# A spectral layer beside a gated linear unit on one Trainium2 core: operand addresses at multiples of 128 bytes, a written order for three engines, one load of x, and another spacing of the spectral tiles

## The chip, the cores and the metric

The kernel runs on one core of a Trainium2 chip. The metric is device time in microseconds (us) for one execution. The engines that matter here are TensorE (PE, matrix products; PEld is its loading of the stationary operand), VectorE (DVE), ScalarE (ACT), GpSimd (POOL, nearly unused) and SyncE (SP), whose queue issues nearly all DMA transfers.

## The reference

From x (2048 rows of 576 floats), normalised by row, two branches are computed and added to x. Everything is float32.

```python
def _A_ref(x, w_r, w_i):
    X = jnp.fft.rfft2(x, axes=(-2, -1))
    X = X * (w_r + 1j * w_i)
    return jnp.fft.irfft2(X, s=(S, D), axes=(-2, -1))

def _B_ref(x, w_gate, w_up, w_down):          # 576 -> 4608 -> 576
    g = jnp.einsum("bsd,df->bsf", x, w_gate)
    u = jnp.einsum("bsd,df->bsf", x, w_up)
    return jnp.einsum("bsf,fd->bsd", _sigmoid(g) * u, w_down)

xn = _layernorm(x, axis=-1)
return x + _A_ref(xn, A_w_r, A_w_i) + _B_ref(xn, B_w_gate, B_w_up, B_w_down)
```

## The kernel before

**Precision.** Each matrix product is made of three: every factor is cut into a rounded high part and a remainder, and high x high, low x high and high x low are accumulated. The high part is a copy on ACT (`hi`, `cut_hi`, `high`), the low part a subtraction on DVE that needs it (`lo`, `cut_lo`, `low`).

**First half: gate and up projections.** The 4608 hidden columns are 36 blocks f of 128. The rows of x are two halves p, each as two chunks of 512. The first two blocks are computed plainly (`plain`); from block 2 on a *unit* (f, p) computes a 2 x 2 block product with seven products P1 to P7 instead of eight (`unit`; `FACTORS` names their factors). A product is seven matmuls with a moving operand of 512 columns (`prod`, L373). The moving operands are the tiles X0... and X1... (halves p = 0 and 1), the stationary ones the weight tiles w. Three PSUM tags take the sums: `bA` and `bE` with two buffers, `bB` with one. The order in a unit: P1 of this unit was made ahead, in the unit before it; ACT copies `bA` to `bB` (L412); P5 to `bE`; P6 onto `bB`, ACT copies it to `h[:,0]` (L416); P2 onto `bA`, ACT takes its sigmoid (L419); P7 onto `bB`, ACT copies it to `h[:,1]` (L422), and DVE adds `bE` to that (L423); P1 of the next unit (`ahead`); P4 onto `bB`, sigmoid (L429); P3 onto `bE`, DVE adds it to `h[:,0]` (L432) and multiplies by the gates (L433). Between the products `beside()` takes one step each of side work written as generators: the weight tiles of the next block (`make_w`; two steps at a time in the units at which f changes, and finished at the fourth call), the sums of h and their store to scratch (`export`, L442), and the factors of w_down and their store to scratch (`make_t`: ACT copy L476, DVE subtraction L478, store L479, through a tile `tP` of tag `tt` with two buffers).

**Second half: down projection and the spectral branch.** The loop over `seq` has 252 steps n = (j, p, k): seven products j of the down projection (`ORDER`), two halves p, 18 blocks k. A step loads one scratch tile `sf` (`fetch`, ten steps ahead), cuts it into `sp` (L617, L621), and makes twelve matmuls `m` of 288 columns (`down`, L1008): four row tiles m by three partial products, with the factor tile `tt` as moving and `sp` as stationary operand. At the last k of a product `evac` adds the four PSUM tiles into the output accumulators `acc` (L946), and `landed` stores finished parts by way of `put` (one half of the rows from SP's queue, the other from ACT's, L711). Beside it the spectral branch runs in three stages of sixteen tiles each, generators again, one step per n (`aside`): `phase1b` (load x, normalise, fold, transposes `pf`, products `pd` and `pa`, store to scratch `sc1`), `phase2` (load from `sc1` and the filter weights w_r and w_i, products `pb` and `pc`, store to `sc2`), `phase3` (load from `sc2`, products `py`, transposes `pz`, products `pe`, added to `acc`). A tile of a stage begins every 4.36 steps, the stages at steps 2, 83 and 166. A tile has 26 matmuls in the first and third stage (six of them transposes) and twelve in the second; those that aren't transposes have 290 columns. Their PSUM tiles come from one tag with two buffers (`pair`). x is loaded twice: into `xb` for the spectral branch, and into `acc`, to which everything is added.

**Addresses.** Pools lie on the left or the right side of the on-chip memory. At the top of the right side stands an unused tile `edge` of eight floats (L155), and below it first `brief` and the X0 tiles, later the ring with `tt`, `sf` and `sp`. X1 and the weight tiles lie on the left. Spectral tiles are two rows of NP = 304 floats, of which 290 are used, so that a second row starts 1216 bytes after the first, nine and a half times 128.

**Order.** Only the opening, before the first plain blocks, is in an order written by hand (`manual_schedule`, DVE and ACT, L518). For all else a planner with its own estimate of durations fixes each engine's order when the kernel is compiled; on the chip an engine then takes its instructions in that order, whatever becomes ready first.

Of the kernel before, what the change touches and what calls it, by code (L numbers as in the profile page):

```python
# [9 lines left out]
F32 = mybir.dt.float32  # L10
# [10 lines left out]
NP = 304  # L21
# [103 lines left out]
def spectral_glu_kernel(ctx: ExitStack, tc: tile.TileContext, x, w_r, w_i, w_gate, w_up, w_down, out):  # L125
# [29 lines left out]
    ctx.enter_context(tc.tile_pool(name="edge", bufs=1, side="right")).tile([P, 8], F32, name="edge")  # L155
# [248 lines left out]
    def unit(u, beside, after):  # L404
# [58 lines left out]
    def make_t(k):  # L463
# [10 lines left out]
        def put(what, src):  # L474
# [5 lines left out]
            yield  # L480

# [141 lines left out]
    def early():  # L623
        for k in range(NPR):
            fetch_t(0, k)
            if k % 2 == 0 and k // 2 < FS:
                fetch(k // 2)
            if k >= 12:
                if k - 12 <= CA:
                    cut_hi(k - 12)  # L630
                if 0 <= k - 13 < CA:
                    cut_lo(k - 13)
            yield
        for n in range(FS, FA):
            fetch(n)
# [3 lines left out]
    make = iter(())  # L639
    for i, u in enumerate(UNITS):  # L640
        f, p = u
# [13 lines left out]
        def beside():  # L655
# [57 lines left out]
    def landed(t):  # L713
# [4 lines left out]
        if pending[t] == 0:  # L718
            put(t, slice(HD, D) if first_rows else slice(0, D))
# [7 lines left out]
    def wide(name, t, bufs=1, dtype=F32):  # L727
        return R["pool"].tile([P, 2, NP], dtype, tag=name, name=f"{name}{t}", bufs=bufs)[:, :, :NQ]

    def left_over(name, t):  # L730
        r = R["pool"].tile([P, 2, 112], F32R, tag=name, name=f"{name}{t}")[:, :, :3 * FR]
        return r, r.rearrange("p e (a b) -> p e a b", a=3)

    def phase1b(t):
# [9 lines left out]
        norm(xb[:, :D], xb[:, :D], t)  # L744
        eo = wide("eo", t)
# [3 lines left out]
        rows_, rp = left_over("rp", t)  # L749
# [30 lines left out]
        ah, al = wide("ah", t, 1, F32R), wide("al", t, 1, F32R)  # L780
# [12 lines left out]
        x1 = wide("x1", t)  # L793
# [3 lines left out]
    def phase2(i):  # L797
        pool, bm = R["pool"], R["bm"]
        kl = 2 * i
        x2 = wide("x2", i, 2)  # L800
        ws = []
        for nm, src in (("wr", w_r), ("wi", w_i)):
            w = pool.tile([P, 592], F32, tag=nm, name=f"{nm}{i}", bufs=2)[:, :2 * KD]
# [10 lines left out]
        h, l = wide("x2h", i, 1, F32R), wide("x2l", i, 1, F32R)  # L814
# [9 lines left out]
        sw, z, t2 = wide("sw", i), wide("z", i, 2), wide("t2", i)  # L824
# [20 lines left out]
        u = wide("u", i, 2)  # L845
# [3 lines left out]
    def phase3(t):  # L849
        pool, di = R["pool"], R["di"]  # L850
        u = wide("u3", t, 2)
# [7 lines left out]
        uh, ul = wide("uh", t, 1, F32R), wide("ul", t, 1, F32R)  # L859
# [10 lines left out]
        rows_, rp = left_over("rp3", t)  # L870
# [44 lines left out]
    def stage1():  # L915
        pool = room("1")
        R["cf"] = cf = pool.tile([P, 2, 5, NP], F32R, name="cf")
        load_r(cf, con["cf"].rearrange("p (e k n) -> p e k n", e=2, k=5))
        yield
# [20 lines left out]
    def evac(what, p, m, b):  # L940
        v = b[:, :HD]
        r1, r2 = acc[tid(p, 0, m)], acc[tid(p, 1, m)]
        c11, c12, c21, c22 = r1[:, :HD], r1[:, HD:], r2[:, :HD], r2[:, HD:]
# [4 lines left out]
        if what == "P1":  # L948
            U[p, m] = u = accp.tile([P, HD], F32, name=f"u{p}{m}")
            nc.scalar.activation(u, v, AF.Copy)  # L950
            add(c11, v)
        elif what == "P2":
            add(c11, v)
        elif what == "P6":
            add(U[p, m], v)
            add(c12, U[p, m])
        elif what == "P7":
            add(U[p, m], v)
            add(c21, U[p, m])
            add(c22, U[p, m])  # L960
        elif what == "P4":
            add(c21, v)
        elif what == "P5":
            w = accp.tile([P, HD], F32, tag="v", name=f"v{p}{m}", bufs=4)
            nc.scalar.activation(w, v, AF.Copy)
            add(c22, w)
            add(c12, w)
            landed(tid(p, 1, m))
        else:
            add(c12, v)  # L970
            landed(tid(p, 0, m))
# [6 lines left out]
    RATE = 4.36  # L978
    B1, B2, B3 = 2, 83, 166
# [72 lines left out]
```

## Time and profile before

| | us |
|---|---|
| median of 3 runs | 1471.11 (1470.16 to 1473.72) |
| profiled execution | 1470.79 |
| its span, first to last instruction | 1469.0 |
| first half, to the first `m` | 887.2 |
| second half, first `m` to the end of the last | 578.0 |
| from there to the last instruction | 3.8 |

The profile is of one execution. A line of a view names line, engine, operation and tiles; `x` is a count. In the table of stretches each engine has its busy time and, in brackets, its instructions; then follow the TensorE clock that was granted (1.00 is full), the mean busy share of the 16 DMA engines, and GB/s. In the waits stand the total, the times and the longest, in us. A matmul's recorded duration overlaps that of the next one, so rates are taken from start to start. On the timeline a row merges neighbours of one kind; its first number is the start, the second the time to the end of the last.

### The profile page before, as it was taken

Reading aid. Unit: us, or ns where it says so; the run is one execution under the profiler, and the core shown is the slowest. Engines: PE = TensorE matmul, PEld = TensorE weight load, DVE = VectorE, ACT = ScalarE, POOL = GpSimd, SP = SyncE. Lnnn points to the kernel's source line nnn. Section 1 sums busy time; section 2 is a strip of 40 time slices with the busy share of each in tenths; the row PEclk is TensorE's granted clock in tenths of the full one; section 3 lists DMA queues with packets and bytes.
Section 4 is the critical chain, followed back from the end, with each engine's and each line's share of the span. In section 5 each row is a group of like instructions: output and inputs, shape, how many; then the busy total and the mean of one; then the engine's idle time right before and its main releaser. Section 6 shows DMA issues by size and latency. Waiting matters only on the chain.

```text
span 1469.0 us, 22700 instructions
## 1 busy us (share of the span) xinstructions
PE 1409.5 (96%) x7804; PEld 1225.3 (83%) x7804; DVE 963.7 (66%) x1808; ACT 707.7 (48%) x1430; POOL 9.5 (1%) x36
## 2 busy tenths in 40 slices
PE   6999999999999999999999998999999999999998
PEld 4888777778777777788888887999999888999998
DVE  6877676758675766656556454666656777566664
ACT  6664454544444454434344332555544555555552
POOL 1000000000000000000000000000000000000000
PEclk9999999999999999999999999999999999999999
DMA  7235556555655565532333259887889999988863
GB/s 191 91 103 194 195 203 217 204 197 192 217 199 201 191 219 209 193 108 92 131 136 115 79 199 323 249 274 234 274 287 306 292 296 297 303 308 277 268 179 91
DMA packets 213619, 306.07 MB, mean 208 GB/s; under 512 B 20480, under 2 KB 98432, under 8 KB 213248
## 3 DMA queue, kind: packets, MB, share of 16 engines
q1 hardware_dynamic: 211440, 302.20, 63.2%
q10 hardware_dynamic: 2064, 2.43, 0.5%
q8 instruction: 61, 1.00, 0.3%
q14 instruction: 54, 0.44, 0.1%
HBM read 187.11 MB, written 117.44 MB: 207 GB/s over the span
## 4 chain that ended last, share of the span: by engine, by line
PE 51%; DVE 15%; DMA 15%; ACT 5%; issue 4%; SPq 4%; DVEq 0%; ACTq 0%
PE m L1008 17%; PE pB L373 11%; PE pE L373 7%; DMA ts<-tP 7%; PE pA L373 7%; DMA sf<-ss 2%; PE pd L778 2%; PE pe L903 2%; DVE w L231 2%; DVE h L433 2%; DMA ss<-h 2%; DVE tP L478 1%; SPq L205 1%; ACT ah L722 1%; DVE w L233 1%
## 5 line engine op out<-in xcount | busy, mean ns | idle before, releaser
L1008 PE MATMUL m<-tt,sp 128*128 128x288 f32 x3024 | 435.5, 298 | 10.7 <-ACT sp L617 7.6
L1008 PEld LDWEIGHTS m<-tt,sp 128*128 128x128 f32 x3024 | 412.1, 189 | 17.2 <-ACT sp L617 11.2
L621 DVE TENSOR_TENSOR sp<-sf,sp 128x512 fp32r<-128x512 f32 x252 | 169.6, 687 | 73.4 <-ACT sp L617 70.3
L617 ACT ACTIVATE sp<-sf 128x512 fp32r<-128x512 f32 x252 | 153.5, 627 | 96.4 <-PE m L1008 48.0
L373 PE MATMUL pA<-X0A,w 128*128 128x512 f32 x518 | 137.1, 400 | 1.8 <-DVE w L211 1.1
L227 ACT ACTIVATE w<-raw 128x384 fp32r<-128x384 f32 x238 | 111.1, 516 | 49.4 <-DVE raw L243 33.5
L373 PE MATMUL pA<-X1A,w 128*128 128x512 f32 x518 | 130.0, 391 | 0.0
L373 PE MATMUL pE<-X0S,w 128*128 128x512 f32 x490 | 125.8, 395 | 0.0
L373 PE MATMUL pB<-X0S,w 128*128 128x512 f32 x476 | 123.0, 396 | 2.7 <-ACT h L416 2.1
L373 PE MATMUL pE<-X1S,w 128*128 128x512 f32 x490 | 123.2, 391 | 0.2 <-DVE h L423 0.2
L373 PEld LDWEIGHTS pA<-X0A,w 128*128 128x128 f32 x518 | 97.7, 190 | 25.8 <-DVE w L211 1.6
L373 PE MATMUL pB<-X1S,w 128*128 128x512 f32 x476 | 119.1, 389 | 0.0
L478 DVE TENSOR_TENSOR tP<-wd,tP 128x288 fp32r<-128x288 f32 x126 | 56.7, 455 | 89.9 <-ACT tP L476 88.8
L373 PEld LDWEIGHTS pA<-X1A,w 128*128 128x128 f32 x518 | 97.1, 188 | 21.3
L373 PEld LDWEIGHTS pB<-X0S,w 128*128 128x128 f32 x476 | 88.4, 187 | 27.4 <-ACT h L416 3.4
L373 PEld LDWEIGHTS pE<-X0S,w 128*128 128x128 f32 x490 | 91.6, 187 | 21.8
L373 PEld LDWEIGHTS pE<-X1S,w 128*128 128x128 f32 x490 | 91.6, 188 | 21.1 <-DVE h L423 1.1
L476 ACT ACTIVATE tP<-wd 128x288 fp32r<-128x288 f32 x126 | 55.2, 442 | 108.1 <-DMA ts<-tP 86.6
L373 PEld LDWEIGHTS pB<-X1S,w 128*128 128x128 f32 x476 | 89.3, 188 | 18.8
L416 ACT ACTIVATE h<-pB 128x512 f32<-128x512 f32 x68 | 40.4, 594 | 131.0 <-PE pB L373 123.3
L423 DVE TENSOR_TENSOR h<-h,pE 128x512 f32<-128x512 f32 x68 | 46.5, 684 | 73.4 <-ACT h L422 73.1
L432 DVE TENSOR_TENSOR h<-h,pE 128x512 f32<-128x512 f32 x68 | 46.4, 683 | 72.4 <-PE pE L373 72.4
(186 smaller groups left out, 1876.9 us busy)
## 6 DMA issues: line engine op xcount, KB each, us to landing
sf<-ss SPq DMA_DIRECT2D x252, 256.0 KB
ss<-h SPq DMA_DIRECT2D x180, 256.0 KB
ts<-tP SPq DMA_DIRECT2D x126, 288.0 KB
tt<-ts SPq DMA_DIRECT2D x126, 288.0 KB
ss<-s SPq DMA_DIRECT2D x72, 256.0 KB
wd<-in_B_w_down SPq DMA_DIRECT2D x36, 288.0 KB
raw<-in_B_w_gate SPq DMA_DIRECT2D x72, 128.0 KB
raw<-in_B_w_up SPq DMA_DIRECT2D x72, 128.0 KB
```

The lines of the kernel that those rows point to most:

```text
L227: nc.scalar.activation(o[:, i, :3, :], src[:, i], AF.Copy)
L231: nc.vector.tensor_tensor(o[:, :, 3:, :], src[:, :, :KT, :], f32(o[:, :, :KT, :]), op=OP.subtract)
L373: nc.tensor.matmul(b, w[:, sw, :], xx[:, sx, :], start=start and j == 0, stop=stop and j == len(STEPS) - 1, skip_group_check=skip)
L416: nc.scalar.activation(h[:, 0], bB, AF.Copy)
L423: nc.vector.tensor_tensor(h[:, 1], h[:, 1], bE, op=OP.add)
L432: nc.vector.tensor_tensor(h[:, 0], h[:, 0], bE, op=OP.add)
L433: nc.vector.tensor_tensor(h, h, g, op=OP.mult)
L476: nc.scalar.activation(t[:, 0], src, AF.Copy)
L478: nc.vector.tensor_tensor(t[:, 1], src, f32(t[:, 0]), op=OP.subtract)
L617: nc.scalar.activation(s[:, 0], SF[n], AF.Copy)
L621: nc.vector.tensor_tensor(SP_[n][:, 1], SF[n], f32(SP_[n][:, 0]), op=OP.subtract)
L1008: nc.tensor.matmul(o, s[:, a, m * P:(m + 1) * P], t[:, b, :], start=k == 0 and i == 0, stop=k == NPR - 1 and i == 2)
```

## The change

- `edge` becomes 24 floats, and NP becomes 320, so that the tiles on the right side and the second rows of the spectral tiles start at multiples of 128 bytes. The tiles `wr`, `wi` and `xb` grow to 608 floats.
- From the third unit to the end PE, DVE and ACT issue in the order in which the program is written. SP's queue stays with the planner.
- With that, places in the written order move: the add of `bE` to `h[:,1]` behind the next unit's P1; one more step of pause in `make_t` after P2, P5 and P6; fewer double steps of `make_w`; the early fetches of `sf` ahead of those of `tt`; in the twin steps of `down` (the first two and the last two k) the matmuls of m = 0, 1 in the first of the two and those of m = 2, 3 in the second; the additions of `evac` over two steps, at the head of the step; P1's addition to `acc` put off to P2.
- `phase1b` loads x into `acc` alone, and normalises from there into one `xb` tile that is cleared once.
- Output stores go to SP's queue alone, but for the last ones.
- The stages begin at steps 3, 72 and 179, with a tile every 3.7, 6.2 and 3.75 steps; in the first and third the order of the tiles changes (upper rows first, then lower rows first).

```diff
-NP = 304
+NP = 320
...
-    ctx.enter_context(tc.tile_pool(name="edge", bufs=1, side="right")).tile([P, 8], F32, name="edge")
+    ctx.enter_context(tc.tile_pool(name="edge", bufs=1, side="right")).tile([P, 24], F32, name="edge")
...
         nc.scalar.activation(h[:, 1], bB, AF.Copy)
-        nc.vector.tensor_tensor(h[:, 1], h[:, 1], bE, op=OP.add)
         beside()
         if after:
             ahead(after)
+        nc.vector.tensor_tensor(h[:, 1], h[:, 1], bE, op=OP.add)
         beside()
...
             nc.sync.dma_start(tsp[ORDER.index(what)][k], f32(t).rearrange("p a d -> p (a d)"))
             yield
+            if what in ("P2", "P5", "P6"):
+                yield
...
+    written = ExitStack()
     for i, u in enumerate(UNITS):
+        if i == 2:
+            written.enter_context(tc.manual_schedule(engines={nc.tensor.engine, nc.vector.engine, nc.scalar.engine}))
...
-            for _ in range(2 if turn else 1):
+            for _ in range(2 if turn and (last or count < 4) else 1):
                 next(make, None)
                 next(soon, None)
             tick()
-            if turn and count == (7 if last else 4):
+            if turn and count == 7:
                 finish(make)
...
-    def put(t, cols):
+    def put(t, cols, both=False):
         for i, r in enumerate(rows(out, t)):
-            (nc.sync, nc.scalar)[i].dma_start(r[:, cols], acc[t][i * N1:(i + 1) * N1, cols])
+            (nc.scalar if both and i else nc.sync).dma_start(r[:, cols], acc[t][i * N1:(i + 1) * N1, cols])
...
-        xb = pool.tile([P, 592], F32, tag="xb", name=f"xb{t}", bufs=2)[:, :D + 2]
-        load_x(xb[:, :D], t)
-        nc.gpsimd.memset(xb[:, D:], 0.0)
+        acc[t] = accp.tile([P, D], F32, name=f"acc{t}")
+        pending[t] = 2
+        load_x(acc[t], t)
+        xb = R["xb"]
...
-        norm(xb[:, :D], xb[:, :D], t)
-        eo = wide("eo", t)
+        norm(xb[:, :D], acc[t], t)
+        eo = wide(pool, "eo", t)
...
         if what == "P1":
             U[p, m] = u = accp.tile([P, HD], F32, name=f"u{p}{m}")
             nc.scalar.activation(u, v, AF.Copy)
-            add(c11, v)
         elif what == "P2":
-            add(c11, v)
+            add(part(0), v)
+            yield
+            add(part(0), U[p, m])
...
-    RATE = 4.36
-    B1, B2, B3 = 2, 83, 166
...
-    for base, phase, n in ((B1, phase1b, HALVES * TPH), (B2, phase2, N2 // 2), (B3, phase3, HALVES * TPH)):
-        for t in range(n):
-            at(base + int(t * RATE), lambda t=t, phase=phase: phase(t))
...
+    UPPER = [tid(p, 0, m) for p in range(HALVES) for m in range(TPC)]
+    LOWER = [tid(p, 1, m) for p in range(HALVES) for m in range(TPC)]
+    for base, rate, stage, phase, ts in ((3, 3.7, stage1, phase1b, UPPER + LOWER), (72, 6.2, stage2, phase2, range(N2 // 2)),
+                                         (179, 3.75, stage3, phase3, LOWER + UPPER)):
+        at(base - 2, stage)
+        for i, t in enumerate(ts):
+            at(base + int(i * rate), lambda t=t, phase=phase: phase(t))
...
-    for i, n in enumerate((0, 3, 6, 9, 13, 17, 21, 25, 32, 40, 48, 56, 64, 72, 80, 88)):
-        t = tid(i // TPC % 2, i // TPH, i % TPC)
-        acc[t] = accp.tile([P, D], F32, name=f"acc{t}")
-        pending[t] = 2
-        loads.setdefault(n, []).append(lambda t=t: load_x(acc[t], t))
...
-            evac(ORDER[j], p, m, M[m])
+            done.append(evac(ORDER[j], p, m, M[m], n == len(seq) - 1))
+
+    done, out_of = [], []
+
+    def emptied():
+        out_of[:] = [g for g in out_of if next(g, out_of) is not out_of]
+        out_of.extend(g for g in done if next(g, done) is not done)
+        done.clear()
...
-        twin = k in (0, NPR - 2)
-        for m in range(TPC):
-            if k not in (1, NPR - 1):
+        emptied()
+        if k in (0, NPR - 2):
+            for m in range(2):
                 down(n, m)
-            if twin:
                 down(n + 1, m)
+        elif k in (1, NPR - 1):
+            for m in range(2, TPC):
+                down(n - 1, m)
+                down(n, m)
+        else:
+            for m in range(TPC):
+                down(n, m)
         active.extend(b() for b in begin.pop(n, []))
         aside()
```

More of the change, by code (lines that the diff above doesn't have):

```diff
@@ L623, in early @@
     def early():
[L624 to L632, printed above, removed]
+        for n in range(20):
+            if n < 2:
+                for i in range(3):
+                    fetch(3 * n + i)
+            else:
+                fetch_t(0, n - 2)
+            if 12 <= n <= 12 + CA:
+                cut_hi(n - 12)
+            if 13 <= n < 13 + CA:
+                cut_lo(n - 13)
             yield
@@ L718, in landed @@
         if pending[t] == 0:
-            put(t, slice(HD, D) if first_rows else slice(0, D))
+            put(t, slice(HD, D) if first_rows else slice(0, D), both)
     def hi(o, src):
@@ L725, in lo, with wide, left_over @@
         nc.vector.tensor_tensor(o, src, f32(h), op=OP.subtract)
[L727 to L731, printed above, removed]
+    def wide(pool, name, t, bufs=1, dtype=F32):
+        return pool.tile([P, 2, NP], dtype, tag=name, name=f"{name}{t}", bufs=bufs)[:, :, :NQ]
+    def left_over(pool, name, t):
+        r = pool.tile([P, 2, 112], F32R, tag=name, name=f"{name}{t}")[:, :, :3 * FR]
         return r, r.rearrange("p e (a b) -> p e a b", a=3)
@@ L792, in phase1b @@
         yield
-        x1 = wide("x1", t)
+        x1 = wide(pool, "x1", t)
         hi(x1, pa[:, :, :NQ])
@@ L799, in phase2 @@
         kl = 2 * i
-        x2 = wide("x2", i, 2)
+        x2 = wide(pool, "x2", i, 2)
         ws = []
         for nm, src in (("wr", w_r), ("wi", w_i)):
-            w = pool.tile([P, 592], F32, tag=nm, name=f"{nm}{i}", bufs=2)[:, :2 * KD]
+            w = pool.tile([P, 608], F32, tag=nm, name=f"{nm}{i}", bufs=2)[:, :2 * KD]
             v = src.rearrange("(k kl) n -> k (kl n)", kl=N2)[:, kl * KD:(kl + 2) * KD]
@@ L918, in stage1 @@
         load_r(cf, con["cf"].rearrange("p (e k n) -> p e k n", e=2, k=5))
+        R["xb"] = xb = pool.tile([P, 608], F32, name="xb")[:, :D + 2]
+        nc.gpsimd.memset(xb[:, D:], 0.0)
         yield
@@ L938, in spectral_glu_kernel, with evac, part @@
     U = {}
-    def evac(what, p, m, b):
+    def evac(what, p, m, b, both):
         v = b[:, :HD]
-        r1, r2 = acc[tid(p, 0, m)], acc[tid(p, 1, m)]
-        c11, c12, c21, c22 = r1[:, :HD], r1[:, HD:], r2[:, :HD], r2[:, HD:]
+        t1, t2 = tid(p, 0, m), tid(p, 1, m)
+        def part(q):
+            return acc[(t1, t2)[q // 2]][:, q % 2 * HD:(q % 2 + 1) * HD]
         def add(o, a):
@@ L950, in evac @@
             nc.scalar.activation(u, v, AF.Copy)
-            add(c11, v)
         elif what == "P2":
-            add(c11, v)
+            add(part(0), v)
+            yield
+            add(part(0), U[p, m])
         elif what == "P6":
             add(U[p, m], v)
-            add(c12, U[p, m])
+            yield
+            add(part(1), U[p, m])
         elif what == "P7":
             add(U[p, m], v)
-            add(c21, U[p, m])
-            add(c22, U[p, m])
+            yield
+            add(part(2), U[p, m])
+            add(part(3), U[p, m])
         elif what == "P4":
-            add(c21, v)
+            add(part(2), v)
         elif what == "P5":
@@ L965, in evac @@
             nc.scalar.activation(w, v, AF.Copy)
-            add(c22, w)
-            add(c12, w)
-            landed(tid(p, 1, m))
-        else:
-            add(c12, v)
-            landed(tid(p, 0, m))
+            yield
+            add(part(3), w)
+            landed(t2)
+            add(part(1), w)
+        else:
+            add(part(1), v)
+            landed(t1, both)
+        yield
     active = []
```

25 lines of the change are left out of this document (13 added, 12 removed).

## The prediction

> **What bounds the kernel now.** I read the page from the top, then the table of stretches, the waits, and the timeline where they fall.
>
> ```profile
> span 1469.0 us, 22700 instructions
> PE 1409.5 (96%) x7804; PEld 1225.3 (83%) x7804; DVE 963.7 (66%) x1808; ACT 707.7 (48%) x1430; POOL 9.5 (1%) x36
> ```
>
> TensorE (PE) is busy 96% of the span, DVE 66%, ACT 48%. So the end moves by two things alone: how far apart matmuls start when nothing is missing, and PE's waits. The profiled execution took 1470.79 us, 1.79 us more than its span; the median of three runs is 1471.11, so the sum below, made against 1470.79, stands 0.3 us under the median.
>
> ```profile
> core 0: us, PE busy (x) PEld busy (x) DVE busy (x) ACT busy (x) POOL busy (x), PEclk, DMA share, GB/s
> 110.00:886.00 776.00, 757.74 (x3253) 606.96 (x3252) 507.12 (x822) 341.71 (x688) 0.10 (x1) 1.00 0.51 177
> 650.00:850.00 200.00, 200.00 (x869) 162.48 (x868) 117.95 (x169) 79.24 (x151) 0.00 (x0) 1.00 0.34 118
> 886.00:920.00 34.00, 28.69 (x198) 27.87 (x198) 14.48 (x25) 9.16 (x18) 0.20 (x2) 0.90 0.99 309
> 920.00:1000.00 80.00, 76.64 (x562) 73.74 (x561) 50.54 (x102) 44.31 (x105) 0.69 (x7) 1.00 0.84 259
> 1000.00:1080.00 80.00, 76.07 (x557) 73.03 (x555) 53.46 (x109) 44.24 (x100) 0.60 (x6) 1.00 0.84 261
> ...
> 1115.00:1150.00 35.00, 31.78 (x228) 30.43 (x227) 24.07 (x52) 18.84 (x32) 0.00 (x0) 1.00 1.03 309
> 1150.00:1200.00 50.00, 45.93 (x318) 43.59 (x317) 36.05 (x78) 26.67 (x45) 0.00 (x0) 0.97 0.99 294
> 1200.00:1270.00 70.00, 65.24 (x462) 61.96 (x462) 52.09 (x112) 40.05 (x70) 0.00 (x0) 1.00 0.96 289
> 1270.00:1330.00 60.00, 60.00 (x453) 59.51 (x452) 35.61 (x66) 30.97 (x64) 0.00 (x0) 1.00 0.92 322
> 1330.00:1400.00 70.00, 70.00 (x536) 70.00 (x535) 47.30 (x93) 39.68 (x87) 0.00 (x0) 1.00 0.80 261
> ```
>
> Four stages show. The units (to 886) leave PE idle 776.00 - 757.74 = 18.3 us, none of it from 650 to 850. Stage 1 of the second half (to about 1110) takes 160 us for 562 + 557 = 1119 matmuls, 143 ns each; stage 2 (1115 to 1270) 155 us for 1008, 154 ns each, with the DMA engines full (0.96 to 1.03); stage 3 needs 70.00 / 536 = 130.6 ns and waits for nothing.
>
> ```profile
> PE pB L373 <- ACT h L422: 15.6, 18, 1.7
> PE pf L759 <- DVE eo L747: 11.2, 12, 5.3
> PE m L1008 <- ACT sp L617: 7.6, 13, 1.4
> ...
> PE pB L373 <- ACT h L416: 2.1, 3, 1.1
> PE m L1008 <- DVE u L946: 1.8, 2, 1.4
> ```
>
> Those are PE's own waits that matter (total, times, longest). The first, on the timeline:
>
> ```profile
> 611.92 0.44 ACT L476 ACTIVATE tP<-wd 128x288 fp32r<-128x288 f32 x1 [4.24 <-DMA ts<-tP]
> 612.27 0.58 ACT L419 ACTIVATE g<-pA 128x512 f32<-128x512 f32 x1
> ...
> 612.75 0.59 ACT L422 ACTIVATE h<-pB 128x512 f32<-128x512 f32 x1
> ...
> 613.39 0.96 PE L373 MATMUL pB<-X1A,w 128*128 128x512 f32 x3 [1.53 <-ACT h L422]
> ```
>
> ACT stood 4.24 us in front of a copy into a `tP` buffer whose store had not landed; the two evacuations queued behind it came late, and P4 could not start into `bB`. It is the place of `L476` in ACT's order that costs, not ACT's load.
>
> **The change part by part.** *Alignment, units.* The edge tile grows from 8 to 24 floats, so all below it on the right side moves down 64 bytes. In the compiled program of before X0's tiles start 64 bytes past a multiple of 128, X1's and the weights' on one; so do `tt` and `sp`. X0 and X1 run the same matmuls:
>
> ```profile
> 700.72 1.75 PE L373 MATMUL pB<-X1S,w 128*128 128x512 f32 x7
> ...
> 702.30 1.79 PE L373 MATMUL pA<-X0A,w 128*128 128x512 f32 x7
> ```
> ```profile
> L373 PE MATMUL pB<-X0S,w x476: 389/394/505, 90.4 to 860.5; 128*128 128x512 f32 x159
> ...
> L373 PE MATMUL pB<-X1S,w x476: 388/389/398, 118.6 to 882.8; 128*128 128x512 f32 x159
> ```
>
> From the X1 product's start to X0's are 1.58 us, 225.7 ns a matmul; medians differ by 394 - 389 = 5 ns, means over all groups of the page by 4 to 9. I take 6 ns for half of the 3556 matmuls of L373, 1778: **-11 us** (bounds 5 and 7: -9 to -12).
>
> The Trainium skill, "SBUF — State Buffer", section Specifications (TRN2), gives 16-byte cachelines; 64 is a multiple of 16, so by it this edit is worth 0 and the sum 11 us less. The 394 against 389 ns disagrees.
>
> *Alignment, second half.* All 3024 `m` matmuls read both operands at 64.
>
> ```profile
> 1269.80 19.37 PE L1008 MATMUL m<-tt,sp 128*128 128x288 f32 x145
> 1289.01 0.30 PE L867 MATMUL py<-uh,ai 128*128 128x290 f32 x1
> ```
> ```profile
> L1008 PE MATMUL m<-tt,sp 128*128 128x288 f32 x3024 | 435.5, 298 | 10.7 <-ACT sp L617 7.6
> ```
> ```profile
> L903 PE MATMUL pe<-dit,z3h 128*128 128x290 f32 x128 | 30.5, 296 | 0.0
> ```
>
> Undisturbed they start 19.21 / 145 = 132.5 ns apart. No row has an aligned 288. One end is 0: the 290-column matmuls, half of whose moving rows start on a multiple of 128 (the other half at 64, NP = 304), last 296 ns, no less than `m`'s 298. The other is the units' 6 ns. The nearest row by length is the 290; but 290 floats touch ten 128-byte pieces from either start, while 288 touch ten from 64 and nine from 0, as 512 touch 17 or 16. So I take 6 ns, as an estimate, and keep 0. For the same reason NP = 320 gets nothing.
>
> *Written order in the units.* make_t's three extra yields put four product slots instead of three between a store and the buffer's next use. A slot is 7 x 230 ns = 1.6 us (200.00 / 869), so 6.4 us against 4.8. The store behind the 4.24 us wait above took 4.55 us to land (the chain of waits, below), which with the subtract ahead of it (0.46 us) fills the 4.8 and not the 6.4.
>
> ```profile
> 607.29 4.55 DMA ts<-tP
> ```
>
> Moving the `bE` add behind the next unit's P1 keeps DVE's other work out from behind an ACT copy, and it is due only before P3, a slot later. PE's 18.3 us of idle go to about 4 by my estimate. Each wait also breaks the overlap of two matmuls (390 ns long, 230 apart: 0.16 us), 23 times, 4 us. **-18 us** (bounds 0, the planner's order being as good, and -22).
>
> *Second half.*
>
> ```profile
> 887.19 20.78 PE L1008 MATMUL m<-tt,sp 128*128 128x288 f32 x156
> ```
> ```profile
> 1450.69 14.47 PE L1008 MATMUL m<-tt,sp 128*128 128x288 f32 x108
> ```
>
> It runs from 887.2 to 1465.2 (first `m` to the end of the last), 578 us for 252 steps of 12 `m`. The new bases end stage 1 at step 72, give stage 2 about 100 steps instead of 70, and stage 3 the last 80. A spectral tile has 26 matmuls in stages 1 and 3 and 12 in stage 2.
>
> Stage 1: 72 x 12 + 16 x 26 = 1280 matmuls at stage 3's 130.6 are 167 us, less 864 x 6 ns = 5 by alignment, plus 4 for waits that stay (the first `x` came late behind the prefetch, 5.3 us): 166. In written order a spectral step has a whole step (12 x 132.5 ns = 1.6 us and more) between producer and consumer, with DVE busy 36.05 / 50.00 = 72% even in stage 2. Single loading of `x` saves 32 loads of 144 KB (`acc`, listed below) here where DMA is at 0.84: counted 0, as are the memsets.
>
> Stage 3: 80 x 12 + 16 x 26 = 1376 x 130.6 = 180, less 6: 174.
>
> Stage 2 is the DMA's.
>
> ```profile
> sf<-ss SPq DMA_DIRECT2D x252, 256.0 KB
> ...
> tt<-ts SPq DMA_DIRECT2D x126, 288.0 KB
> ...
> sc<-u SPq DMA_DIRECT2D x16, 290.0 KB
> ...
> wr<-in_A_w_r SPq DMA_DIRECT2D x32, 144.5 KB
> ...
> acc<-in_A_x SPq DMA_DIRECT2D x32, 144.0 KB
> ```
>
> A step moves one `sf` and half a `tt`, 400 KB (0.41 MB); a tile one read and one write of 290 KB and four weight loads of 144.5 KB, 1158 KB (1.19 MB). At 4.36 steps a tile that is 0.68 MB a step, at about 295 GB/s (share 0.99) 2.3 us; the lighter stretch at 1270 moves 322 GB/s at 0.92, 350 at full, so the 0.41 MB are worth 1.17 us and a tile 4.9. At 6.2 steps a tile the need is 1.17 + 0.78 = 1.95 us a step, against PE's 12 x 132.5 + 12 x 132.5 / 6.2 = 1.85 without and 1.77 with alignment. So DMA still ends last: 100 x 1.95 = 195, and alignment is worth nothing here.
>
> The Trainium skill, "Perfetto Trace Analysis", section Engine Utilization, puts the peak of HBM at 358 GB/s for a core and lets a single one exceed it; by that 0.60 MB fits in 1.77 us, stage 2 takes 177 and the sum is 18 us lower. The full share at 289 to 309 GB/s speaks against it.
>
> Sum 166 + 195 + 174 = 535; with 5 us for waits of the written order 540: **-38 us**. ACT loses its output DMAs to SP; the last tile keeps both queues, so the tail of 3.8 us stays. At the other edits (order of prefetches, P1's add deferred to P2) nothing waits: 0.
>
> Together -11 - 18 - 38 = -67: 1470.8 - 67 = **1404 us**.
>
> **The rivals.**
> *Written order gives half back.* ACT and DVE now block where the planner had moved things around: a `tP` copy still waits for its store, `sw` for `pb`. For: ACT stood 4.24 us in one such wait. Against: the added yields. Half of -18 and -38 kept: 1471 - 11 - 28 = 1432.
> *Alignment does nothing for 288 columns.* Speaks for it the 296 against 298. Stage 1 and 3 lose 11: 1415; if X0 too gains nothing, 1426.
> *DMA isn't the bound in stage 2.* Stage 2 stretched runs at PE's pace, 18 us less: 1386. For: PE's recorded waits there name ACT, and the DMA share of 0.96 has slack. Against: 1.03.
> *Slower.* PE in written order cannot take `m` ahead of a spectral step that isn't ready. There are 16 x (3 + 2 + 3) = 128 such steps. If each waited 0.9 us, as the 12 `pf` waits did (11.2 / 12), +119 and 19 of broken overlap: 1542. It ends slower from 67 / 128 = 0.5 us a step. Against: the whole step of lead, engines at 72% and less.
> *The order isn't what it says* (the two schedules nearly equal): alignment alone, -11 - 11: 1449.
>
> **How the numbers follow.** Forecast 1404: 0.48. Half back: 0.18. No gain for 288: 0.10. DMA not the bound: 0.13. Orders equal: 0.04. Slower: 0.05. No change, gains and losses cancelling: 0.02. The forecast's own range takes the bounds of its terms: 1390 to 1424. Low end: stage 2 by PE and all waits gone, -12 - 22 - 61 = 1376. High end: the half-back case with no gain for 288 columns, 1443. So 1376 to 1443 leaves out the slower case, no change, the equal orders and tails. A measurement of this kernel tells about 0.3% from no change: faster 0.93 (all but the last two), same 0.02, slower 0.05.
>
> **What would show it.** X0's medians at X1's 389 ns. An undisturbed run of `m` at about 126 ns instead of 132.5. Waits of `pB` for `h` down from 15.6 us to a few, ACT's wait for `ts<-tP` in units much shorter. Stage 1 at about 130 ns a matmul; stage 2 with a DMA share near 1.0 and PE waiting for `sp` behind `sf`. Wrong it would be if spectral steps show PE waits one by one, or ACT's evacuations start late in most units.

## The result, and the profile after

The changed kernel is slower: 1493.44 us (median of 4 runs, 1491.6 to 1495.55) against 1472.28 (4 runs), a ratio of 1.0145 (95% interval 1.0124 to 1.0167). The forecast was 1404 us, faster. The profiled execution took 1494.7 us. From the page of the kernel after, its span and the busy times:

```profile
span 1492.9 us, 22678 instructions
PE 1410.8 (95%) x7804; PEld 1239.1 (83%) x7804; DVE 965.7 (65%) x1808; ACT 699.6 (47%) x1430; POOL 8.1 (1%) x21
```

The same 7804 matmuls are busy for about the same time as before (1409.5 us), but the span is 24 us longer, so TensorE (PE) stands still more. The table of stretches of the kernel after (columns as in the prediction) tells where:

```profile
110.00:400.00 290.00, 273.55 (x1164) 221.18 (x1162) 183.82 (x291) 120.36 (x243) 0.00 (x0) 0.97 0.47 161
400.00:650.00 250.00, 236.23 (x996) 191.47 (x997) 161.70 (x261) 106.32 (x218) 0.00 (x0) 0.96 0.51 173
650.00:850.00 200.00, 188.72 (x800) 152.82 (x799) 129.72 (x211) 85.26 (x175) 0.00 (x0) 0.97 0.51 174
...
921.00:1103.00 182.00, 171.59 (x1282) 169.93 (x1281) 116.67 (x237) 97.52 (x223) 0.00 (x0) 0.97 0.87 273
1103.00:1304.00 201.00, 190.55 (x1386) 186.53 (x1385) 136.14 (x284) 102.81 (x177) 0.00 (x0) 0.99 0.92 288
1304.00:1490.00 186.00, 183.26 (x1384) 182.49 (x1383) 112.58 (x225) 89.68 (x201) 0.00 (x0) 1.00 0.70 219
```

From 650 to 850, where PE was busy all the time with 869 matmuls before, it now makes 800, with 11.3 us idle and a granted clock of 0.97 instead of 1.00. The first `m` starts at 920.8 us instead of 887.2: the units lost 33.6 us. The second half gained a little: 568.3 us instead of 578.0, with step 72 reached after 182.0 us (before 182.4), step 172 after another 201.3 (214.0), the end after 185.0 more (181.6).

PE's and ACT's waits in the units of the kernel after (total, times, longest):

```profile
PE pB L373 <- ACT pB L412: 39.2, 7, 5.9
PE pE L373 <- DVE w L231: 2.3, 1, 2.3
PE pB L373 <- ACT h L422: 1.1, 2, 0.7
...
ACT tP L476 <- DMA wd<-in_B_w_down: 41.9, 7, 6.4
ACT tP L476 <- DVE wd L487: 21.1, 18, 1.2
...
ACT tP L476 <- DMA ts<-tP: 7.2, 7, 1.9
```

The wait that the prediction set out to remove, `pB` for `h` (15.6 us, 18 times), is down to 1.1. In its place stand seven waits of over 5 us each, and ACT has seven, too: for `wd`, the rows of w_down that `make_t` works on. One of them on the timeline of the kernel after (rows of ACT's L476 and L412, DVE's L478, the `wd` load, and PE):

```profile
199.67 1.76 PE L373 MATMUL pE<-X1S,w 128*128 128x512 f32 x7
...
202.37 0.45 DVE L478 TENSOR_TENSOR tP<-wd,tP 128x288 fp32r<-128x288 f32 x1
202.89 0.38 SPq L468 DMA_DIRECT2D wd<-in_B_w_down  x1
206.14 0.44 ACT L476 ACTIVATE tP<-wd 128x288 fp32r<-128x288 f32 x1 [5.71 <-DMA wd<-in_B_w_down]
206.49 0.58 ACT L412 ACTIVATE pB<-pA 128x512 f32<-128x512 f32 x1
...
207.13 3.35 PE L373 MATMUL pB<-X1S,w 128*128 128x512 f32 x7 [5.69 <-ACT pB L412]
210.28 1.84 PE L373 MATMUL pA<-X1A,w 128*128 128x512 f32 x7
```

Read it from below. PE stood 5.69 us in front of P6, which adds onto what L412 copies to `pB`. L412 stood behind `make_t`'s copy L476 on ACT. That copy waited for a load that could be issued (at 202.89) only when a DVE subtraction had ended its work on the same buffer (at 202.82), and that was usable 3.2 us later. And the wait costs twice: the seven matmuls after it span 3.35 us where seven take 1.76, that is, they start at about half the rate.

The Trainium skill, "TensorE: Matmul & The Clock Gate", Part 1, has the array fall to half its clock after an idle window of about 3.4 us and come back after as long a busy one. These rows agree (a wait of 5.69 us, then half rate for seven matmuls); the last section shows a limit of it.

In the second half, the waits of the kernel after:

```profile
PE pf L766 <- DVE eo L754: 7.5, 1, 7.5
PE pb L829 <- ACT x2h L728: 3.7, 4, 1.6
PE pb L829 <- DVE x2l L731: 2.8, 8, 0.4
```

The first spectral tile stands before its x, and stage 2's tiles before x2. Line numbers are those of each kernel: L1020 here is the `m` matmul of L1008, and in the experiments they shift by a few.

### The profile page after: what moved, and what is told of

Same layout as the page of the kernel before. It is cut to its first block, busy times and chain, and to the rows that moved or that the text cites. A ratio compares the mean times of both kernels' runs of the same rounds, so it can differ in the third digit from the quotient of the medians.

```text
span 1492.9 us, 22678 instructions
## 1 busy us (share of the span) xinstructions
PE 1410.8 (95%) x7804; PEld 1239.1 (83%) x7804; DVE 965.7 (65%) x1808; ACT 699.6 (47%) x1430; POOL 8.1 (1%) x21
## 4 chain that ended last, share of the span: by engine, by line
PE 75%; DMA 8%; DVE 5%; ACT 2%; issue 2%; SPq 1%; DVEq 0%; ACTq 0%
PE pB L373 22%; PE m L1020 18%; PE pA L373 14%; PE pE L373 13%; DMA x<-sc 2%; PE pe L910 2%; PE pd L785 2%; DMA wd<-in_B_w_down 2%; DVE sp L623 1%; DMA acc<-in_A_x 1%; PE py L874 1%; PE pa L798 1%; DMA sf<-ss 1%; DVE h L433 1%; DMA ss<-h 1%
## 5 line engine op out<-in xcount | busy, mean ns | idle before, releaser
L1020 PE MATMUL m<-tt,sp 128*128 128x288 f32 x3024 | 426.6, 298 | 4.8 <-DVE u L958 1.6
L1020 PEld LDWEIGHTS m<-tt,sp 128*128 128x128 f32 x3024 | 411.5, 190 | 6.2 <-ACT zh L728 2.6
L373 PE MATMUL pB<-X1S,w 128*128 128x512 f32 x476 | 130.2, 416 | 39.2 <-ACT pB L412 39.2
L373 PEld LDWEIGHTS pB<-X1S,w 128*128 128x128 f32 x476 | 95.3, 202 | 62.4 <-ACT pB L412 42.2
L373 PE MATMUL pA<-X1A,w 128*128 128x512 f32 x518 | 133.4, 398 | 0.0
L231 DVE TENSOR_TENSOR w<-raw,w 128x512 fp32r<-128x512 f32 (+1 forms) x102 | 79.3, 778 | 81.3 <-ACT w L227 76.5
L227 ACT ACTIVATE w<-raw 128x384 fp32r<-128x384 f32 x238 | 117.3, 515 | 20.1 <-PE pE L373 11.4
L373 PEld LDWEIGHTS pA<-X1A,w 128*128 128x128 f32 x518 | 100.6, 195 | 22.7
L432 DVE TENSOR_TENSOR h<-h,pE 128x512 f32<-128x512 f32 x68 | 46.6, 686 | 101.8 <-PE pE L373 101.7
L429 ACT ACTIVATE g<-pB 128x512 f32<-128x512 f32 x68 | 40.7, 598 | 130.3 <-PE pB L373 130.3
L478 DVE TENSOR_TENSOR tP<-wd,tP 128x288 fp32r<-128x288 f32 x126 | 57.2, 454 | 58.0 <-ACT tP L476 56.9
```

The source lines that it names most:

```text
L227: nc.scalar.activation(o[:, i, :3, :], src[:, i], AF.Copy)
L231: nc.vector.tensor_tensor(o[:, :, 3:, :], src[:, :, :KT, :], f32(o[:, :, :KT, :]), op=OP.subtract)
L373: nc.tensor.matmul(b, w[:, sw, :], xx[:, sx, :], start=start and j == 0, stop=stop and j == len(STEPS) - 1, skip_group_check=skip)
L429: nc.scalar.activation(g[:, 1], bB, AF.Sigmoid)
L432: nc.vector.tensor_tensor(h[:, 0], h[:, 0], bE, op=OP.add)
L478: nc.vector.tensor_tensor(t[:, 1], src, f32(t[:, 0]), op=OP.subtract)
```

## The experiments

All medians beside the place where the time lies; "second half" is first `m` to the end of the last in the profiled run.

| kernel | median us | ratio to before (95%) | first `m` | second half |
|---|---|---|---|---|
| before | 1472 | | 887.2 | 578.0 |
| after | 1493.44 | 1.0145 (1.0124 to 1.0167) | 920.8 | 568.3 |
| after, no pauses | 1440.97 | 0.9779 (0.9755 to 0.9804) | 870.5 | 565.5 |
| after, planner's order | 1436.94 | 0.9752 (0.9732 to 0.9773) | 885.3 | 547.3 |
| the same, even spacing | 1446.07 | 0.9829 (0.9814 to 0.9844) | 884.7 | 555.2 |
| the same, even spacing, x twice | 1467.97 | 0.9968 (0.9956 to 0.998) | 883.4 | 579.2 |
| no pauses, written order in the units alone | 1425.33 | 0.9689 (0.9671 to 0.9708) | 871.5 | 547.4 |
| the same, X0 moved by 384 bytes | 1416.53 | 0.9612 (0.9589 to 0.9634) | 862.5 | 548.7 |

### The pauses and the order

**After, without `make_t`'s pauses.**

```diff
-            if what in ("P2", "P5", "P6"):
-                yield
```

> The changed kernel without the extra pauses in make_t after P2, P5 and P6. Theory 1 (the pauses moved the last read of a wd buffer two product slots later, while the next make_t starts after a fixed 14 calls, so its first ACT copy meets a load that has not landed, and the copy of bA to bB stands behind it): the seven waits of pB for ACT's L412, 39.2 us in all, go to under 5 us, with them the slow clock after each (mean granted clock from 0.979 to 0.995), about 1435 us. Rival (any copy of make_t in ACT's written order holds up the evacuations, whichever buffer it waits for): the waits come back behind tP's stores, 15 us or more of waits of pB remain, and the time is above 1450 us.

1440.97 us, 52 less than after. ACT's wait for `wd` is gone. The waits behind `tP`'s stores do come back on ACT, as the rival had it, but PE waits only 2.4 us for L412 (waits of this kernel, PE's and ACT's):

```profile
PE pB L373 <- ACT pB L412: 2.4, 4, 0.8
...
ACT tP L476 <- DMA ts<-tP: 28.3, 29, 1.8
```

The units run at full clock (the stretch of the units of this kernel):

```profile
110.00:870.00 760.00, 754.03 (x3255) 610.81 (x3254) 511.74 (x821) 337.40 (x689) 0.10 (x1) 1.00 0.53 182
```

PE idles 6.0 us there (760.00 - 754.03), against 18.3 before. So the written order, with the places moved for it, does help the units, by 17 us (870.5 against 887.2), and the three pauses undo that three times over.

**All pauses in front**, behind P1, so that the distance between the last use of the second of `make_t`'s two `wd` buffers and its next use is again what it was.

```diff
-            if what in ("P2", "P5", "P6"):
-                yield
+            if what == "P1":
+                for _ in range(3):
+                    yield
```

> The kernel after with make_t's three pauses all behind the first block (P1) and none behind P2, P5 and P6: as many slots in all, but the next make_t's second copy, the first to read the second weight buffer, comes three slots later too. Theory (the last subtraction, P4's, frees that buffer in the very slot in which the next make_t's P2 copy wants it filled again; the distance is what counts): the seven waits of over 5 us are gone, units as without pauses, 1437 to 1445 us. Rival (any make_t that lasts 21 slots collides with the next): 1480 to 1495 us.

1494.07 us (1.0145, 1.012 to 1.0169): the theory missed. The seven long waits did vanish, as it said, but another came (waits of this kernel in the units):

```profile
PE pB L373 <- ACT pB L412: 37.2, 22, 2.1
...
ACT tP L476 <- DVE wd L488: 41.5, 12, 3.5
ACT tP L476 <- DMA raw<-in_B_w_up: 21.0, 6, 3.7
```

and its timeline shows why:

```profile
263.09 1.23 DVE L433 TENSOR_TENSOR h<-h,g 128x1024 f32<-128x1024 f32 x1
264.23 0.45 DVE L488 TENSOR_TENSOR wd<-wd 128x288 f32<-128x288 f32 x1
264.76 0.44 ACT L476 ACTIVATE tP<-wd 128x288 fp32r<-128x288 f32 x1 [3.46 <-DVE wd L488]
265.12 0.58 ACT L412 ACTIVATE pB<-pA 128x512 f32<-128x512 f32 x1
...
265.75 3.04 PE L373 MATMUL pB<-X0S,w 128*128 128x512 f32 x7 [1.86 <-ACT pB L412]
```

P5's copy follows at once on the subtraction that makes its source (L488). With the pauses in front it falls into the slot that ends a unit, where DVE first has to do `h` times the gates, which waits for the unit's last product, and where the next thing on ACT is L412, the one copy that PE waits for. This happens in each of the 18 `make_t` (12 of the waits stand under L488, 6 under a load of `raw`). So where a slot lies in the unit matters as much as how many there are, and this kernel could not tell which of the two the pauses of the change had hit.

**All pauses behind P6**: P5's copy keeps its slot, only P4, the last block, comes three slots later.

```diff
-            if what in ("P2", "P5", "P6"):
-                yield
+            if what == "P6":
+                for _ in range(3):
+                    yield
```

> The kernel after with make_t's three pauses all behind P6, none behind P2 and P5. Everything up to P6 stands in the slots that it has without pauses (P5's copy too); only P4 comes three slots later, in the slot in which the next make_t's P2 copy wants P4's buffer filled again. Theory (the second weight buffer is loaded again too late, which costs the seven waits of over 5 us and what follows them): the seven waits are there, units end at 905 or later, 1475 to 1495 us. Rival (the buffer costs little; the pauses cost because they move P5's copy to a worse slot of the unit, as the 18 waits for DVE L488 had it with all pauses in front): 1438 to 1446 us, units end at 870 to 874.

1490.99 us (1.0138, 1.011 to 1.0166), first `m` at 916.6, and the waits of the change are back, as many and as long:

```profile
PE pB L373 <- ACT pB L412: 37.4, 7, 5.8
...
ACT tP L476 <- DMA wd<-in_B_w_down: 44.4, 9, 6.3
```

That settles it: it is the buffer. The second `wd` buffer holds B21 and B22. Its last reader is P4's subtraction, in the 18th slot of the generator; its next first reader is the following `make_t`'s P2 copy, in its seventh (not its first copy, as the first expectation had it). Where two `make_t` begin one block apart (14 slots; `4 + k * 8 // 5` gives 7 such pairs among 17), that copy comes in slot 14 + 7 = 21, three slots or 4.8 us after the subtraction, enough for the 3.8 us from 202.37 to 206.14 above. With three pauses the subtraction is in slot 21 as well. The seven waits are these seven pairs.

**After, in the planner's order throughout.**

```diff
-        if i == 2:
-            written.enter_context(tc.manual_schedule(engines={nc.tensor.engine, nc.vector.engine, nc.scalar.engine}))
```

> The changed kernel with all its edits but without the written order: the planner orders PE, DVE and ACT again. If written order is what makes the late wd load cost (theory 1 in its strict form: the planner would move the copy behind the evacuations), the waits of pB for L412 are gone and the units take about as long as before (777 us): about 1450 us. If the pauses alone cost, whatever the order, the seven waits stay: about 1490 us.

1436.94 us, 13 less than expected. The planner moves the `make_t` copies off the critical place, pauses and all (first `m` at 885.3), and its second half takes 547.3 us, 18 less than the written order's 565.5. The same three parts of the second half, first in the planner's order, then in the written one without pauses:

```profile
885.00:1061.00 176.00, 170.71 (x1283) 168.31 (x1282) 117.67 (x236) 100.41 (x223) 0.00 (x0) 1.00 0.90 282
1061.00:1247.00 186.00, 184.89 (x1377) 183.56 (x1376) 132.29 (x277) 103.88 (x172) 0.00 (x0) 1.00 0.96 301
1247.00:1433.00 186.00, 185.28 (x1395) 184.03 (x1393) 119.39 (x231) 95.58 (x204) 0.00 (x0) 1.00 0.73 230
```
```profile
870.00:1051.00 181.00, 171.61 (x1280) 169.83 (x1279) 115.84 (x235) 97.41 (x223) 0.00 (x0) 0.97 0.88 275
1051.00:1252.00 201.00, 190.78 (x1388) 186.81 (x1387) 136.56 (x286) 103.17 (x176) 0.00 (x0) 0.99 0.93 289
1252.00:1436.00 184.00, 183.24 (x1387) 182.90 (x1386) 112.50 (x225) 90.16 (x201) 0.00 (x0) 1.00 0.70 220
```

The difference lies in the first part (5 us) and in stage 2 (15 us), where the written order has PE idle for 10.2 us and the planner for 1.1.

**No pauses, written order in the units alone.** `written.close()` stands ahead of the second half instead of behind it.

> The kernel after without the extra pauses (1440.97 us), with the written order ended before the second half, so that the planner orders that half. Theory (the written order wins some 15 us in the units and loses 18 us in the second half, and the two are independent): units as without pauses (first product at 870), second half 547 to 550 us, 1421 to 1427 us in all, ratio 0.966 to 0.970. Rival (what the planner wins in the second half hangs on how the units left the queues: with the units in written order it gives only part): 1432 to 1441 us, second half 558 to 566.

1425.33 us, second half 547.4: the two effects add, as the theory had it.

**Longer lead for x2**, in the written order without pauses: six yields instead of three between the load of x2 and its first copy in `phase2`, and stage 3 three steps later, ending at the same step.

```diff
+        yield
+        yield
+        yield
...
-                                         (179, 3.75, stage3, phase3, LOWER + UPPER)):
+                                         (182, 3.55, stage3, phase3, LOWER + UPPER)):
```

> The kernel after without the extra pauses, written order throughout, with each spectral tile of stage 2 loaded three steps earlier before its first use (six pauses instead of three between load and copy; stage 3 begins three steps later at a rate of 3.55 so that it ends at the same step). Theory (the written order loses time in stage 2 because ScalarE stands behind the load of x2: 49.0 us in 12 waits): these waits shrink below 10 us, steps 72 to 172 take 188 to 193 us instead of 201, 1428 to 1434 us in all. Rival (the load is not what delays TensorE in stage 2; the order itself or the transfers are): steps 72 to 172 stay at 198 or more, 1437 to 1443 us.

1437.29 us (0.9762, 0.9743 to 0.9781), steps 72 to 172 in 193.3 us (201.0 without the lead). The steps come out at the theory's edge, the total at the rival's: ACT's wait for x2 shrank from 49.0 to 1.7 us, which returned 8 of the 15 us of stage 2; of these the total kept 4 (the last 80 steps took 2.2 us more than without the longer lead). PE's waits of this kernel in the second half name two that are left:

```profile
PE pf L764 <- DVE eo L752: 6.7, 1, 6.7
PE m L1021 <- DVE u L959: 5.4, 4, 1.8
```

The first is the first tile's x, whose load SP issues behind that of the constants `cf`; the second an eviction's addition that stands late in DVE's order.

### The spacing and x

**Planner's order with the old even spacing.**

```diff
-    for base, rate, stage, phase, ts in ((3, 3.7, stage1, phase1b, UPPER + LOWER), (72, 6.2, stage2, phase2, range(N2 // 2)),
-                                         (179, 3.75, stage3, phase3, LOWER + UPPER)):
+    for base, rate, stage, phase, ts in ((3, 4.36, stage1, phase1b, UPPER + LOWER), (83, 4.36, stage2, phase2, range(N2 // 2)),
+                                         (166, 4.36, stage3, phase3, LOWER + UPPER)):
```

> The kernel after without the written order (1436.94 us), with the old even spacing of the spectral tiles (4.36 steps throughout, stage 2 from step 83, stage 3 from 166). Theory (in stage 2 the transfers end last, and the wider spacing is worth what the prediction took for it): the second half loses 15 us or more, 1452 us or more, and the loss is in stage 2's steps. Rival (x loaded once is what shortens the second half; the spacing is worth little): 1434 to 1442 us.

1446.07 us, between the two: the spacing is worth 9.1 us (1446.07 - 1436.94). The loss is in stage 2's steps, as the theory had it, but smaller. The stretch of steps 83 to 166 in this kernel:

```profile
1075.00:1249.00 174.00, 166.62 (x1196) 161.17 (x1195) 128.73 (x272) 98.02 (x163) 0.00 (x0) 0.99 0.97 296
```

PE idles 7.4 us here, and there is a matmul every 145 ns; with the wider spacing PE idles 1.1 us in its stage 2, with a matmul every 135 ns (186.00 / 1377, above).

**The same with x loaded twice**, `xb` with two buffers and `acc` at the old steps.

```diff
-        acc[t] = accp.tile([P, D], F32, name=f"acc{t}")
-        pending[t] = 2
-        load_x(acc[t], t)
-        xb = R["xb"]
+        xb = pool.tile([P, 592], F32, tag="xb", name=f"xb{t}", bufs=2)[:, :D + 2]
+        load_x(xb[:, :D], t)
+        nc.gpsimd.memset(xb[:, D:], 0.0)
```

> The kernel after without the written order and with the even spacing (1446.07 us), with x loaded twice as before (a buffer of its own for the spectral tile, the sums' copy at the old steps). Theory (the second half became shorter, 578 to 555 us with the same spacing and planner, because 32 loads of 144 KB are gone: 4.7 MB at about 0.3 MB per us are 15 us): 1457 to 1464 us. Rival (the loads of x were covered; the gain came from the evictions' deferred additions and the output's queue): 1443 to 1449 us.

1467.97 us: x once is worth 22 us, more than the 15 estimated for its bytes. The first 83 steps in both, x once above:

```profile
885.00:1075.00 190.00, 187.08 (x1410) 185.16 (x1408) 126.83 (x250) 108.20 (x234) 0.00 (x0) 1.00 0.89 281
```
```profile
883.00:1091.00 208.00, 195.43 (x1416) 188.03 (x1415) 127.05 (x250) 105.22 (x234) 1.50 (x15) 0.98 0.86 266
```

Counted from the first `m` to step 83, it is 207.6 us instead of 190.7: 17 of the 24 us by which the second half grew lie here (7 more in stage 2's steps), with PE idle 12.6 us instead of 2.9 and the clock at 0.98, though the DMA share is no higher. PE's waits with x twice are, over the second half, for `sp` (10.0 us, 12 times) and `eo` (8.5, 11 times), whose loads share SP's queue with the 32 that are gone; whether it is their bytes or their places in that queue was not tried apart. The rest of the change that this kernel keeps (addresses, put-off additions, output queue, order of the tiles, pauses) is worth 4 us together against before (ratio 0.9968), which leaves the rival little.

### The addresses

**Before, with the new addresses alone** (`edge` 24 floats, NP = 320, the longer `w` and `xb`).

> The kernel before with the addresses of the change alone (edge of 24 floats, NP = 320, 608 floats in wr, wi and xb). By the prediction X0's matmuls come to 227 ns apart and m to 126: 11 + 18 us less in the rate, 1449 us. Theory 2 (the distance of X0 from X1 has nothing to do with 128-byte pieces; in the changed kernel X0 stands at multiples of 128 and its matmuls last as long as before): no change within 0.3%, 1472 us.

1470.09 us, ratio 0.9983 (0.9968 to 0.9997): at most 0.3%. X0 stands on multiples of 128 and is hardly faster (tile rows of this kernel: min, median, max ns):

```profile
L373 PE MATMUL pB<-X0S,w x476: 387/392/505, 90.8 to 860.9; 128*128 128x512 f32 x159
...
L373 PE MATMUL pB<-X1S,w x476: 388/389/441, 119.0 to 883.2; 128*128 128x512 f32 x159
```

By the 16-byte lines of the Trainium skill, "SBUF — State Buffer", section Specifications (TRN2), this edit was worth nothing, and that ratio agrees; they do not account for X0 being slower than X1.

**Before, X0 on the left and X1 on the right** (the pools exchanged, and the halves of the last two blocks with them).

```diff
-    xps = [first.enter_context(tc.tile_pool(name="x0", bufs=1, side="right", reuse_waits="tile")), pool1("x1")]
+    xps = [pool1("x0"), first.enter_context(tc.tile_pool(name="x1", bufs=1, side="right", reuse_waits="tile"))]
```

> The kernel before with the tiles of p = 0 on the left side and those of p = 1 on the right (and p = 1 first in the last four units, so that the right side comes free in time). Theory 3a (a moving operand on the right, with its weights on the left, is what costs 6 ns a matmul): now X1's medians are 394 ns and X0's 389. Theory 3b (it is the work beside the units of p = 0 that slows their matmuls): X0 stays at 394, X1 at 389. The time in both is that of before, 1472 us within 10 us, as the same number of matmuls is on each side.

1472.18 us (1.0002, 0.9987 to 1.0017), and the medians change places, X1 now the slow one:

```profile
L373 PE MATMUL pB<-X0S,w x476: 387/389/504, 89.8 to 879.5; 128*128 128x512 f32 x159
...
L373 PE MATMUL pB<-X1S,w x476: 392/394/500, 117.7 to 857.2; 128*128 128x512 f32 x159
```

So it is the place and not the data. Three more kernels ask which property of the place.

**Before, the right side 448 bytes further**, so that X0 stands at the same remainder modulo 2048 (896) as X1.

```diff
-.tile([P, 8], F32, name="edge")
+.tile([P, 120], F32, name="edge")
```

> The kernel before with 112 more floats (448 bytes) of padding at the far end of the right side, nothing else: X0's tiles move by 448 bytes, so that they stand at the same offset modulo 2048 as X1's. Theory (the 6 ns that X0's matmuls take more come from the side of the memory on which a tile stands): nothing changes, ratio 0.997 to 1.003, X0 stays near 394 ns and X1 near 389 in the matmuls on pA, pB, pE. Rival (they come from the offset within 2 KB): X0 falls to 389 ns, 1778 matmuls x 6 ns = 11 us less, ratio 0.9925.

1465.77 us (0.9963, 0.9947 to 0.9979). It is not the side: X0 falls to 389.

```profile
L373 PE MATMUL pB<-X0S,w x476: 387/389/504, 89.4 to 857.6; 128*128 128x512 f32 x159
```

6 us are gained and not 11: PE waits for `h` (L422) 20.2 us between 110 and 880 us instead of 14.9.

**Before, the left side 448 bytes further**: weights and X1 move, X0 stays.

```diff
+    ctx.enter_context(tc.tile_pool(name="rim", bufs=1)).tile([P, 112], F32, name="rim")
```

> The kernel before with 112 floats (448 bytes) of padding at the near end of the left side: the weights w and X1's tiles move by 448 bytes, so that X1 stands at 1344 modulo 2048 like X0; X0 stays where it was. Theory (the offset of the moving tile within 2 KB decides by itself): X1's matmuls rise from 389 to 394 ns and X0's stay, 1778 x 6 ns = 11 us more, 1478 to 1485 us. Rival (what counts is the distance between the weights and the moving tile): X0's distance becomes that of the padded right side, X1's is kept: X0 falls to 389, 1461 to 1467 us.

1466.09 us (0.9962, 0.9945 to 0.9978), and both are fast, the rival's outcome:

```profile
L374 PE MATMUL pB<-X0S,w x476: 387/389/504, 90.2 to 857.6; 128*128 128x512 f32 x159
...
L374 PE MATMUL pB<-X1S,w x476: 388/389/395, 118.2 to 879.8; 128*128 128x512 f32 x159
```

X0 has not moved, and X1 now has the remainder (1344) at which X0 was slow. What counts is the distance between the two sides, on one of which the weights lie.

**Before, the right side 64 bytes off the good place** (`edge` 104 floats).

> The kernel before with the right side's padding at 104 floats: X0's tiles stand 64 bytes (modulo 2048) from the place at which their matmuls fell to 389 ns, and no longer on a multiple of 128. Theory (only the coarse distance between weights and moving tile counts, 128-byte multiples do not): X0 stays at 389 ns, 1463 to 1469 us. Rival (the exact distance counts, or the multiple of 128): X0 at 392 to 395 ns, 1469 to 1475 us.

1468.34 us (0.9985, 0.9969 to 1.0002), X0 mostly back near 394, so the distance has to fit closely:

```profile
L373 PE MATMUL pB<-X0S,w x476: 387/392/505, 89.7 to 861.2; 128*128 128x512 f32 x159
```

**Everything that paid, together**: the planner for the second half, the units in written order without pauses, and `edge` at 120 floats (384 bytes beyond the change's).

> The units in written order without the pauses, the planner for the second half (1425.33 us), with the right side's padding at 120 floats, so that X0's tiles stand at 896 modulo 2048. Theory (the padding's gain in the units adds): X0 at 389 ns, units 1778 x 6 ns = 11 us shorter less what the waits take back, 1414 to 1420 us. Rival (with TensorE nearly free of waits the units are bound by ACT and DVE in their written order, and faster matmuls turn into waits): 1422 to 1427 us.

1416.53 us (0.9612, 0.9589 to 0.9634), units 9 us shorter than with `edge` at 24. From the page of this kernel:

```profile
PE 1383.3 (98%) x7804; PEld 1226.5 (87%) x7804; DVE 968.1 (68%) x1808; ACT 705.6 (50%) x1430; POOL 8.0 (1%) x21
```

It beats both kernels, by 56 us and 77 us.

## Why the prediction was wrong

**Written order in the units, -18: the step that failed.** The prediction said that "make_t's three extra yields put four product slots instead of three between a store and the buffer's next use". That is right for `tP`: ACT's wait for `ts<-tP` is 7.2 us in the kernel after and 28.3 without the pauses. But it was not needed, as PE idles only 6.0 us in the units without them, and a pause that lengthens one distance shortens another. The same three slots were taken from between the last read of `wd` and its next fill, and the prediction counted no such distance for `wd`. The term came out at +34; without the pauses it is -17, as sized. In the planner's order the units with the pauses take no longer than before (885.3 against 887.2), since it puts ACT's copies where they fit; only the written order makes the pauses exact. So the rival that had the written order give half back was right about the mechanism (ACT blocked in order, PE behind it), and far too mild.

**Alignment in the units, -11, and in the second half, another 11 within the -38: nothing of it came.** All the addresses together changed the time by a ratio of 0.9983, 0.3% at most. The evidence was X0's 394 ns against X1's 389, read as 64 bytes of misalignment. X0 and X1 differ in more than that, and exchanging and shifting them shows the distance to the other side to be the cause. The 288-column `m`, supposed to fall from 132.5 to about 126 ns, keeps its mean of 298 ns on the page of the kernel after:

```profile
L1020 PE MATMUL m<-tt,sp 128*128 128x288 f32 x3024 | 426.6, 298 | 4.8 <-DVE u L958 1.6
```

The rival that gave alignment nothing (1426) was right. Of the 11 us of the units, 9 can be had, by another 384 bytes.

**Second half, -38: measured -10.** Its terms: the first 72 steps 166 (measured 182), the next 100 steps 195 (201), the last 80 steps 174 (185). x's single loading was counted 0 and is worth 22 us. The spacing is worth 9. With these and the planner the half takes 547 us, 7 more than predicted: stages 1 and 3 were sized at 130.6 ns a matmul, less the alignment, and the planner's rows have 133 (170.71 / 1283 and 185.28 / 1395). In stage 2 the prediction had DMA end last at 1.95 us a step; the planner's run does 186 us there with PE busy for 184.89 of them: the rival "DMA isn't the bound in stage 2" was right. PE's pace without the alignment, which the prediction put at 1.85 us a step, is what was measured (1.86). The loss is the written order's, counted as 5 us and measured as 18: 8 of it by the loads of x2, which three slots of lead do not cover (the longer lead gave these steps the 8 us back, though the total only 4), some 5 by the first x (read from the waits, not tried); what the other 5 are is open. The whole step between producer and consumer that the prediction counted on did not cover a load: ACT waited 49.0 us for x2 in the run without the pauses.

**The slower rival** had the spectral steps wait on PE one by one, from 0.5 us a step. In the kernel after PE's three waits in the second half that are shown above add up to 14 us, so that is not how it became slower; the loss came in the units, where no rival had one.

## What to carry to other kernels

Before an engine's order is written out, count for every buffer that is filled again the slots from its last read to its next first use, a load's flight included, and look which evacuation stands behind the instruction that would wait; a pause that widens one distance narrows the next. A planner may be kept for the half in which loads and many small steps interleave, and the written order for the half with a fixed rhythm: here the mixture beat either alone. When two operands run at different rates, exchange and shift them before naming the cause.

## What the runs showed of the hardware

- **A wait on PE can cost more than itself, even a short one.** In the kernel with all pauses in front, PE has 18 waits of about 1.9 us for L412; after 9 of them six to eight of the matmuls that follow start at about half the rate (the row at 265.75 above: seven in 3.04 us), after the other 9 none, as here:

```profile
192.40 1.91 PE L373 MATMUL pB<-X0S,w 128*128 128x512 f32 x7 [1.86 <-ACT pB L412]
```

  Where the wait falls decides it. In the units of this trace the granted clock drops to 0.50 for 3.41 us at a time, and these drops begin whole multiples of 3.413 us apart, as on a fixed grid. In each of the 9 cases PE was idle for 1.86 us or more (0.55) of one such stretch, and the next stretch ran at half clock; in the other 9 no stretch held more than 1.74 us (0.51) of the wait. In the row at 265.75, PE was busy for 1.55 of the 3.41 us up to 266.12; the clock was 0.50 for the next 3.41 us, then 1.00 again.

  The 3.4 us of the Trainium skill's page on the clock gate ("TensorE: Matmul & The Clock Gate", Part 1) is thus no lower limit for an idle time here: these were about 2 us.
- **The distance between the moving tile and the other side of the memory is worth 5 ns in a matmul of 512 columns.** Moving either side by 448 bytes removes it (394 to 389 ns; from one start to the next 233 to 227 ns); 64 bytes beside the good place most of it is back (392 to 394). Whether the weights or something else on the left side is the partner, and which distances are good, was not tried further.
